# One batch for the last matrix product of a gated mix, with the top-8 taken from the gate pass's own rows and the chosen rows transposed by DMA

## The chip, the cores and the metric

The kernel runs on one core of a Trainium2 chip. The metric is the device time of one launch in microseconds; lower is better. The times of one version differ by about 1 us from run to run, so small differences are judged by ratios with an interval.

Engine names in the profile: PE is the tensor engine (PEld its weight loads), DVE the vector engine, ACT the scalar engine, POOL the GpSimd engine, SP the engine whose queue issues most loads. "L771" is a line of that version's program. Line numbers shift by a few from version to version.

## The reference, cut to what matters

```
x = A_x                                             # 2048 tokens x 1024, bf16
g = sigmoid((x * gate_w).sum(-1))                   # a gate for each token
a = 2 * Re(scan(x @ B_bar^T) @ C^T) + x * Dskip     # a diagonal complex recurrence over the tokens
b = x; for the 8 tokens with the largest x @ w_r:
      b[token] += silu(x_sel @ w_gate) * (x_sel @ w_up) @ w_down * sigmoid(r_sel)
out = g * a + (1 - g) * b
```

There are two streams. The large one is `a`: a product with B (called s1 below, PSUM tiles `vps`), a scan on DVE, and a product with C (s2, PSUM tiles `zps`). The small one is `b`: choose 8 tokens, gather their rows, and run three matrix products on 8 rows. They read 22 MB of weights. The small stream is threaded between the matmul groups of the large one.

## The kernel before

The program emits matmul groups in a fixed order. Functions in a list `at((block, position), f)` are run after a given group. A position therefore fixes only where something stands in each engine's queue; when it runs is decided by waits. These are the parts that the change and the argument touch:

```python
xpool = ctx.enter_context(tc.tile_pool(name="xpool", bufs=4))   # 4 x tiles in flight
...
def mul_e(b):        # DVE scales x tile b, POOL's queue stores it
    ...
    nc.gpsimd.dma_start(out2d[b * P:(b + 1) * P, :], xt[:])
def skip_d(k):       # DVE: xd = x * Dskip for the two tiles of block k
    for b in (2 * k, 2 * k + 1): ...
def rows(k):
    for b in (2 * k - 2, 2 * k - 1):
        mul_e(b)
        if b + 4 < NTT:
            load_x(b + 4)          # into the buffer that tile b's store must first leave
...
def load_w():        # SP loads a weight slot into each buffer that came free
def moe_slot(s):     # the matmuls of weight slot s; then its buffer is free, and load_w()
...
def fin_b():         # DVE scales the 8 rows y
def scatter_upd():   # POOL adds them to out in DRAM, then SP reads the last tiles back ("ul")
...
at((3, 2.3), lambda: (rows(2), skip_d(2), dve_scan(3, 0, 8)))
at((3, 6.5), lambda: (skip_d(3), dve_post(3, 0, 8)))          # dve_post makes H, which s2 reads
at((9, 0.1), lambda: last_m(1))
at((9, 2.95), lambda: (fin_b(), scatter_upd(), last_scan(1)))
pos = [(3, 4.9)] * 2 + ... + [(8, 1.9)] * 4 + [(9, 2.9)] * 3  # where each weight slot is used
```

`rows(2)` stores x tiles 2 and 3 and then loads tiles 6 and 7 into the same two buffers. `skip_d(3)` needs tiles 6 and 7. The last two entries of `pos` are the product with w_down, called y, in two batches.

Of the kernel before, what the change touches and what calls it, by code (L numbers as in the profile page):

```python
# [9 lines left out]
ALU = mybir.AluOpType  # L10
# [14 lines left out]
def kernel(  # L25
# [45 lines left out]
    X = {}  # L71
    BT = [const.tile([P, KD, NP_], BF16, name=f"BT{pl}") for pl in range(2)]
    CT = [const.tile([P, NCT, D], BF16, name=f"CT{pl}") for pl in range(2)]
# [60 lines left out]
    nc.gpsimd.iota(ramp[:], pattern=[[1, LC]], base=0, channel_multiplier=0, allow_small_or_imprecise_dtypes=True)  # L134
    jrow8 = small.tile([8, NTT, 8], F32, name="jrow8")
    nc.gpsimd.iota(jrow8[:], pattern=[[P, NTT], [0, 8]], base=0, channel_multiplier=0, allow_small_or_imprecise_dtypes=True)
    M = {}
    rg = small.tile([P, KD, 32], BF16, name="rg")
    nc.gpsimd.memset(rg[:], 0.0)
    ones16 = small.tile([NTT, 8], BF16, name="ones16")  # L140
    nc.gpsimd.memset(ones16[:], 1.0)
    for i, v in enumerate((B_w_r, gate_w)):
# [290 lines left out]
    nc.vector.tensor_scalar(out=rs4[:, 1, 0, :], in0=rot[:, 1, 1, :], scalar1=-1.0, scalar2=None, op0=ALU.mult)  # L433

    s1x(1, 0)
    tab_arg(1)
    tab_abs(1)
    vb_ps = ps_m.tile([P, 2, NCT], BF16, name="vb_ps", tag="m")
    for i in range(2):
        nc.tensor.transpose(vb_ps[:, i, :], vrow[:, 3 + i, :], ident[:NCT, :NCT])  # L440
    nc.vector.tensor_copy(rg[:, :, 0:2].rearrange("p k t -> p t k"), vb_ps[:])
# [36 lines left out]

    rcb = small.tile([P, NTT], BF16, name="rcb")
    gcol = small.tile([P, NTT], F32, name="gcol")  # L480
# [10 lines left out]
    def gate_cols():  # L491
        zt = ps_m.tile([P, 4, P], BF16, name="zt", tag="m")
        for tq in range(4):
            nc.tensor.transpose(zt[:, tq, :], M["zrb"][:, tq * P:(tq + 1) * P], ident[:])
        zv = zt[:].rearrange("p t (j s) -> p j t s", s=32)
        zb = small.tile([P, NTT], BF16, name="zb")
        nc.scalar.copy(out=zb[:].rearrange("p (j t) -> p j t", t=4), in_=zv[:, :, :, 1])
        gb = sigm(small, zb[:], [P, NTT], "gc")
        nc.scalar.copy(out=gcol[:], in_=gb[:])
        nc.scalar.copy(out=rcb[:].rearrange("p (j t) -> p j t", t=4), in_=zv[:, :, :, 0])  # L500
        ob = small.tile([P, NTT], BF16, name="ob")
        nc.scalar.activation(out=ob[:], in_=gb[:], func=ACT.Copy, scale=-1.0, bias=1.0)
        nc.scalar.copy(out=omgcol[:], in_=ob[:])
        M["aT"] = small.tile([P, NFC // 4, 4, 32], BF16, name="aT", tag="va")
        nc.gpsimd.memset(M["aT"][:], 0.0)
# [11 lines left out]
    def sel_a():  # L517
        rT_ps = ps_m.tile([NTT, P], BF16, name="rT_ps", tag="m")
        nc.tensor.transpose(rT_ps[:], rcb[:], ident[:])
        rT = rowp.tile([NTT, P], F32, name="rT", tag="row8")  # L520
        nc.scalar.copy(out=rT[:], in_=rT_ps[:])
        M["rT"] = rT

    def sel_a2():
        rT = M["rT"]
        mA = rowp.tile([NTT, NSEL], F32, name="mA")
        iA = rowp.tile([NTT, NSEL], U32, name="iA")
        nc.vector.max(out=mA[:], in_=rT[:])
        nc.vector.max_index(out=iA[:], in_max=mA[:], in_values=rT[:])
        iAf = rowp.tile([NTT, NSEL], F32, name="iAf")  # L530
        nc.vector.tensor_copy(iAf[:], iA[:])
        mm = rowp.tile([NTT, 2, NTT, NSEL], BF16, name="mm", tag="mg")
        eyeb = ident[:NTT, :NTT].unsqueeze(2).to_broadcast([NTT, NTT, NSEL])
        nc.vector.tensor_tensor(out=mm[:, 0], in0=mA[:].unsqueeze(1).to_broadcast([NTT, NTT, NSEL]), in1=eyeb, op=ALU.mult)
        nc.vector.tensor_tensor(out=mm[:, 1], in0=iAf[:].unsqueeze(1).to_broadcast([NTT, NTT, NSEL]), in1=eyeb, op=ALU.mult)
        M["mm"] = mm

    def sel_b():
        mm = M["mm"]
        fl_ps = ps_m.tile([NSEL, 2, NTT * NSEL], F32, name="fl_ps", tag="m")  # L540
        for k in range(2):
            nc.tensor.matmul(fl_ps[:, k, :], lhsT=ones16[:], rhs=mm[:, k].rearrange("k j s -> k (j s)"), start=True, stop=True)
        fl = rowp.tile([NSEL, 2, NTT * NSEL], F32, name="fl", tag="gr0")
        nc.scalar.copy(out=fl[:], in_=fl_ps[:])
        M["fl"] = fl

    def sel_b2():
        fl = M["fl"]
        cv = fl[:, 0, :]
        ci = rowp.tile([NSEL, NTT * NSEL], F32, name="ci", tag="mg")  # L550
        nc.vector.tensor_tensor(out=ci[:], in0=fl[:, 1, :], in1=jrow8[:].rearrange("p j s -> p (j s)"), op=ALU.add)
        gm = rowp.tile([NSEL, NSEL], F32, name="gm")
        kx = rowp.tile([NSEL, NSEL], U32, name="kx")
        nc.vector.max(out=gm[:], in_=cv)
        nc.vector.max_index(out=kx[:], in_max=gm[:], in_values=cv)
        kxf = rowp.tile([NSEL, NSEL], F32, name="kxf")
        nc.vector.tensor_copy(kxf[:], kx[:])
        dtmp = rowp.tile([NSEL, 2, NSEL], F32, name="dtmp")
        nc.vector.tensor_tensor(out=dtmp[:, 0, :], in0=kxf[:], in1=ident[:NSEL, :NSEL], op=ALU.mult)
        nc.vector.tensor_tensor(out=dtmp[:, 1, :], in0=gm[:], in1=ident[:NSEL, :NSEL], op=ALU.mult)  # L560
        dsel = rowp.tile([NSEL, 2], F32, name="dsel")
        nc.vector.reduce_sum(out=dsel[:], in_=dtmp[:], axis=AX)
        eq = rowp.tile([NSEL, NTT * NSEL], F32, name="eq", tag="gr1")
        nc.vector.tensor_scalar(out=eq[:], in0=ramp[:NSEL, 0:NTT * NSEL], scalar1=dsel[:, 0:1], scalar2=None, op0=ALU.is_equal)
        nc.vector.tensor_tensor(out=eq[:], in0=eq[:], in1=ci[:], op=ALU.mult)
        tokf = rowp.tile([NSEL, 1], F32, name="tokf")
        nc.vector.reduce_sum(out=tokf[:], in_=eq[:], axis=AX)
        idx_c = small.tile([NSEL, 1], I32, name="idx_c")
        nc.vector.tensor_copy(idx_c[:], tokf[:])
        M["idx_c"] = idx_c  # L570
        xsel = rowp.tile([NSEL, D], BF16, name="xsel", tag="row8")
        nc.gpsimd.indirect_dma_start(out=xsel[:], out_offset=None, in_=x2d, in_offset=bass.IndirectOffsetOnAxis(ap=idx_c[:, :1], axis=0))
        M["xsel"] = xsel
        M["dsel"] = dsel
    def sel_c():
        xsel = M["xsel"]
        xselT_ps = ps_m.tile([P, KD, NSEL], BF16, name="xselT_ps", tag="m")
        for dc in range(KD):
            nc.tensor.transpose(xselT_ps[:, dc, :], xsel[:, dc * P:(dc + 1) * P], ident[:NSEL, :NSEL])
        xselT = M["xsel32"]  # L580
        nc.scalar.copy(out=xselT[:, :, 0:NSEL], in_=xselT_ps[:])
        M["xselT"] = xselT
        M["rs_e"] = sigm(rowp, M["dsel"][:, 1:2], [NSEL, 1], "rs")
# [40 lines left out]
    def load_w():  # L624
        while nload[0] < NS and free_w:
            s = nload[0]
            tag = free_w.pop(0)
            if s < NGU // 2:
                h, dc = divmod(s, KD)
# [3 lines left out]
            else:  # L633
                w = const.tile([P, 2, 2, D], BF16, name="wd", tag=tag)
                for i in range(2):
# [10 lines left out]
    def moe_slot(s):  # L646
        for i in range(2):
            moe_item(2 * s + i, wq[s][0][:, i])
        free_w.append(wq.pop(s)[1])
        load_w()  # L650
# [190 lines left out]
    at((3, 1.9), sel_c)  # L841
    at((3, 3.9), sel_d)
    at((3, 1.2), lambda: dve_m(3, 0, 8))
    at((3, 2.3), lambda: (rows(2), skip_d(2), dve_scan(3, 0, 8)))
    at((3, 4.2), lambda: (sel_c2(), sel_d2()))
    at((3, 2.2), lambda: rows_e(2))
# [10 lines left out]
    at((5, 3.4), lambda: fin(6))  # L857
    at((5, 2.6), lambda: (dve_m(5, 0, 8), dve_scan(5, 0, 8)))
    at((5, 2.5), lambda: skip_d(4))
    at((6, 2.2), lambda: skip_x(8))  # L860
# [22 lines left out]
    at((8, 2.5), lambda: fin(10))  # L883
    at((9, 2.92), fin_a)
    at((8, 3.95), lambda: fin(11))
    at((9, 0.0), lambda: (skip_d(7), last_post(0, 0, NCT)))
    at((9, 0.1), lambda: last_m(1))
    at((9, 2.95), lambda: (fin_b(), scatter_upd(), last_scan(1)))
    at((9, 2.5), lambda: fin(12))
# [3 lines left out]

    pos = [(3, 4.9)] * 2 + [(4, 1.9)] * 3 + [(5, 1.9)] * 3 + [(6, 1.9)] * 3 + [(6, 5.9)] * 3 + [(7, 0.9)] * 2 + [(8, 1.9)] * 4 + [(9, 2.9)] * 3
    for s in range(NW // 2):
# [10 lines left out]
    for n, (m, k) in enumerate(blocks):  # L906
        free_w.extend(fill.get(n, ()))
        load_w()
        if k is None:
# [45 lines left out]
```

## Time and profile before

| | before |
|---|---|
| time, median of the first 3 runs | 249.81 us (249.35 to 250.25) |
| span of the profiled run | 248.3 us |
| PE busy | 242.7 us, 98% |
| DVE busy | 227.0 us, 91% |
| PE's clock | full (mean granted 1.000) |

The page's busy part (busy us, share of the span, instructions) of the kernel before:

```profile
PE 242.7 (98%) x1414; PEld 115.6 (47%) x1414; DVE 227.0 (91%) x231; ACT 117.4 (47%) x203; POOL 33.6 (14%) x50
```

A busy PE is not by itself a PE at its limit, so the order matters. These are lines of the chain of waits of the kernel before, in order of time: start, length (both in us), engine, tile, line, and number of instructions.

```profile
66.83 3.45 PE zps L771 x16
70.28 0.15 PE rT_ps L519
...
101.93 0.28 PE xselT_ps L579 x8
...
109.23 0.27 PE zs_ps L595 x8
109.50 3.56 PE vps L266 x16
...
207.16 1.86 PE y L672 x64
...
226.39 1.42 PE y L672 x48
...
238.28 6.96 PE zps L787 x48
```

From 61 to 245 us the chain is PE alone, one piece after another. A group of 16 large matmuls takes 3.45 us in a stream. After an interruption by matmuls with smaller weights (128 x 8 for `zs_ps`) it takes 3.56 us; after one with weights of 128 x 128 (`zt`, which stands just before the first line shown, and `aT_ps` at 203.3 us) it takes 3.45 us. The tiny transposes (`rT_ps`, `xselT_ps`), the gate product `zs_ps` and the two `y` pieces are the interruptions that the change attacks.

A line of a timeline gives start, length, engine, line, operation, tile, and in brackets the idle time before and what ended it.

Two waits of DVE at the end of the kernel before, from its view of waits (who waited for whom; us in total, times, longest):

```profile
DVE xt L760 <- DMA ul<-out_dram: 2.6, 1, 2.6
DVE yc L696 <- ACT yc L691: 2.6, 1, 2.6
```

### The profile page before, as it was taken

To read this page: it belongs to the slowest core of one execution; us is meant where nothing else is said; L and a number is where in the kernel's file an instruction comes from. 1 tells how busy PE (TensorE), PEld (TensorE's weight loads), DVE (VectorE), ACT (ScalarE), POOL (GpSimd) and SP (SyncE) were. 2 spreads that over 40 slices of the span, in tenths; PEclk is the share of its full clock that TensorE was granted. 3 is DMA by queue.
4 is the path that set the end of the run, shared out by engine and by line. 5 is a ranking of instruction groups with operands and counts; after the bars stand their busy time and mean duration, and the time that the engine had idled before them with its cause. 6 is when DMAs were issued, how large, how long until landed. Compare 5 with 4: busy or idle time off the path is not lost.

```text
span 248.3 us, 3608 instructions
## 1 busy us (share of the span) xinstructions
PE 242.7 (98%) x1414; PEld 115.6 (47%) x1414; DVE 227.0 (91%) x231; ACT 117.4 (47%) x203; POOL 33.6 (14%) x50
## 2 busy tenths in 40 slices
PE   7899999999999999999999999999999999999995
PEld 5664444444444444444444444444444445445453
DVE  0899999999999999999999999999999999995954
ACT  3599973333345322282354571235267445537421
POOL 4000000000100003151402050100100211011810
PEclk9999999999999999999999999999999999999999
DMA  7999999999760000077976989877599972993053
GB/s 170 214 201 213 223 228 202 261 220 255 225 220 0 3 0 0 7 187 210 340 212 225 343 252 300 279 240 291 156 313 317 374 157 59 308 309 45 3 118 96
DMA packets 64193, 48.25 MB, mean 194 GB/s; under 512 B 49568, under 2 KB 51232, under 8 KB 64176
## 3 DMA queue, kind: packets, MB, share of 16 engines
q1 hardware_dynamic: 59120, 37.23, 55.5%
q0 software_dynamic: 3424, 7.90, 14.8%
q10 hardware_dynamic: 1632, 2.89, 3.8%
q8 instruction: 11, 0.18, 0.3%
q14 instruction: 6, 0.05, 0.1%
HBM read 27.55 MB, written 8.40 MB: 145 GB/s over the span
## 4 chain that ended last, share of the span: by engine, by line
PE 84%; DVE 7%; DMA 4%; SPq 3%; issue 0%; ACT 0%; DVEq 0%
PE zps L771 42%; PE vps L266 32%; DMA X<-in_A_x_dram 4%; PE zps L787 3%; PE pgu L660 3%; SPq L80 2%; PE vps L282 1%; PE y L672 1%; DVE U L302 1%; DVE U L313 1%; DVE H L340 1%; DVE U L338 1%; DVE H L336 1%; PE zr L487 1%; DVE S2tab L252 1%; DVE Ctab L251 1%
## 5 line engine op out<-in xcount | busy, mean ns | idle before, releaser
L771 PE MATMUL zps<-CT,H 128*128 128x512 bf16 x480 | 105.5, 379 | 0.0
L266 PE MATMUL vps<-X,BT 128*128 128x512 bf16 x480 | 105.1, 379 | 0.0
L266 PEld LDWEIGHTS <-BT 128*128 128x128 bf16 x480 | 46.4, 98 | 56.6 <-PE pgu L660 0.7
L771 PEld LDWEIGHTS <-H 128*128 128x128 bf16 x480 | 46.2, 98 | 56.3 <-issue 1.5
L313 DVE TENSOR_TENSOR_SCAN U<-d,U 128x2048 bf16<-128x2048 f32 (+2 forms) x22 | 62.0, 2860 | 1.0 <-DVE U L304 0.5
L273 ACT CAST V<-vps 128x512 bf16<-128x512 f32 x60 | 32.2, 588 | 56.3 <-PE vps L266 56.3
L776 ACT ACTIVATE ot<-zps,gcol 128x512 bf16<-128x512 f32 x30 | 20.6, 687 | 54.1 <-PE zps L771 54.1
L797 POOL DMA_DIRECT2D out_dram<-ot x14 | 13.0, 931 | 34.4 <-ACT ot L776 24.0
L303 DVE TENSOR_TENSOR V<-V,nTi 128x4096 bf16<-128x4096 bf16 (+2 forms) x11 | 16.7, 1517 | 0.5
L304 DVE TENSOR_TENSOR U<-U,V 128x4096 bf16<-128x4096 bf16 (+2 forms) x11 | 16.7, 1516 | 0.4
L302 DVE TENSOR_TENSOR U<-V,T2tab 128x4096 bf16<-128x4096 bf16 (+2 forms) x11 | 16.6, 1509 | 0.4
L338 DVE TENSOR_TENSOR U<-U,S2tab 128x4096 bf16<-128x4096 bf16 x7 | 16.0, 2292 | 0.2
L340 DVE TENSOR_TENSOR H<-H,U 128x4096 bf16<-128x4096 bf16 x7 | 16.0, 2292 | 0.2
L336 DVE TENSOR_TENSOR H<-U,Ctab 128x4096 bf16<-128x4096 bf16 x7 | 16.0, 2283 | 0.0
L745 ACT CAST zps<-xd 128x512 f32<-128x512 bf16 (+1 forms) x25 | 14.2, 575 | 3.2 <-ACT xt L732 2.9
L709 POOL DMA_DIRECT2D xt<-in_A_x_dram x12 | 7.1, 592 | 62.7 <-DMA out_dram<-xt 31.5
L732 ACT ACTIVATE xt<-xt,omgcol 128x1024 bf16<-128x1024 bf16 x12 | 13.8, 1146 | 0.0
L371 DVE TENSOR_TENSOR_SCAN U<-D,U 128x1024 bf16<-128x1024 f32 x4 | 8.9, 2271 | 0.1
L282 PE MATMUL vps<-X,BT 128*128 128x256 bf16 x64 | 7.5, 273 | 0.9 <-DMA X<-in_A_x_dram 0.6
L727 DVE TENSOR_TENSOR xd<-xt,Dbc 128x1024 bf16<-128x1024 bf16 x12 | 7.7, 682 | 0.3 <-ACT V L273 0.3
L282 PEld LDWEIGHTS <-BT 128*128 128x128 bf16 x64 | 6.1, 98 | 2.4 <-issue 0.7
L660 PE MATMUL pgu<-wgu,xsel 128*32 128x448 bf16 x128 | 7.2, 354 | 0.0
(161 smaller groups left out, 152.7 us busy)
## 6 DMA issues: line engine op xcount, KB each, us to landing
wgu<-in_B_w_gate_dram SPq DMA_DIRECT2D x16, 448.0 KB, 6.5
wgu<-in_B_w_up_dram SPq DMA_DIRECT2D x16, 448.0 KB, 5.8
wd<-in_B_w_down_dram SPq DMA_DIRECT2D x12, 512.0 KB, 7.6
out_dram<-ot POOLq DMA_DIRECT2D x14, 256.0 KB, 5.8
xt<-in_A_x_dram POOLq DMA_DIRECT2D x12, 256.0 KB, 4.2
out_dram<-xt ACTq DMA_DIRECT2D x10, 256.0 KB, 5.3
xt<-in_A_x_dram SPq DMA_DIRECT2D x4, 256.0 KB, 3.5
out_dram<-xt POOLq DMA_DIRECT2D x4, 256.0 KB, 3.4
```

What stands on the lines that cost most here:

```text
L266: nc.tensor.matmul(o, lhsT=BT[pl][:, dc, ct * P:(ct + 1) * P], rhs=X[m][:, dc, k0 * LC:k1 * LC], start=(dc == 0), stop=(dc == KD - 1))
L273: nc.scalar.copy(out=V[k][:, :, ct, :], in_=vp[m, ct][:, :, kk, :])
L282: nc.tensor.matmul(vps[:, pl, c, :], lhsT=BT[pl][:, dc, ct * P:(ct + 1) * P], rhs=X[0][:, dc, k * LC:(k + 1) * LC], start=(dc == 0), stop= ...
L302: nc.vector.tensor_tensor(out=u, in0=v, in1=T2tab[:, :, c0:c1, :], op=ALU.mult)
L303: nc.vector.tensor_tensor(out=v, in0=v, in1=bc(nTi, c0, c1), op=ALU.mult)
L304: nc.vector.tensor_tensor(out=u, in0=u, in1=V[k][:, ::-1, c0:c1, :], op=ALU.add)
L313: nc.vector.tensor_tensor_scan(out=fl, data0=d0[:, c0:c1, :].rearrange("p c t -> p (c t)"), data1=fl, initial=0.0, op0=ALU.mult, op1=ALU.add)
L336: nc.vector.tensor_tensor(out=h, in0=g, in1=bc(Ctab, c0, c1), op=ALU.mult)
L338: nc.vector.tensor_tensor(out=g, in0=g, in1=S2tab[:, :, c0:c1, :], op=ALU.mult)
L340: nc.vector.tensor_tensor(out=h, in0=h, in1=G[k][:, ::-1, c0:c1, :], op=ALU.add)
L771: nc.tensor.matmul(zps[:], lhsT=H[k][:, pl, ct, tl * P:(tl + 1) * P], rhs=CT[pl][:, ct, dsl], start=(fresh and ct == 0 and pl == 0), stop= ...
L776: nc.scalar.activation(out=ots[b][:, dsl], in_=zps[:], func=ACT.Copy, scale=gcol[:, b:b + 1])
```

## The change

Its intent has two halves. The **y half** does the product with w_down in one batch, with B's space as room for weights once B has been used, and puts the chosen rows' gate product beside it. The **selection half** takes the top-8 directly from the router rows of the gate pass (4 rows of 512 instead of 16 rows of 128, which needed a transpose on PE), merges 32 instead of 128 candidates with one matmul instead of two, and transposes the gathered rows by DMA instead of by PE. The diff, cut to its core:

```diff
     def sel_a():
-        rT_ps = ps_m.tile([NTT, P], BF16, name="rT_ps", tag="m")
-        nc.tensor.transpose(rT_ps[:], rcb[:], ident[:])
-        rT = rowp.tile([NTT, P], F32, name="rT", tag="row8")
-        nc.scalar.copy(out=rT[:], in_=rT_ps[:])
+        rT = rowp.tile([P, 2 * LC], F32, name="rT", tag="row8")
+        nc.scalar.copy(out=rT[:], in_=M["zrb"][:])
 ...
+        M["xsel"] = rowp.tile([32, D], BF16, name="xsel", tag="row8")
+        nc.gpsimd.memset(M["xsel"][:], 0.0)
 ...
     def sel_c():
-        for dc in range(KD):
-            nc.tensor.transpose(xselT_ps[:, dc, :], xsel[:, dc * P:(dc + 1) * P], ident[:NSEL, :NSEL])
-        nc.scalar.copy(out=xselT[:, :, 0:NSEL], in_=xselT_ps[:])
+        nc.sync.dma_start_transpose(xselT[:], xsel[:])
 ...
-    at((3, 3.9), sel_d)
+    at((8, 3.88), sel_d)
 ...
-    at((9, 2.92), fin_a)
+    at((8, 3.92), fin_a)
-    at((9, 2.95), lambda: (fin_b(), scatter_upd(), last_scan(1)))
+    at((9, 0.95), lambda: last_scan(1))
+    at((9, 0.15), lambda: (sel_c2(), sel_d2(), fin_b(), scatter_upd()))
 ...
-    pos = ... + [(8, 1.9)] * 4 + [(9, 2.9)] * 3
+    pos = ... + [(8, 3.9)] * 7
 ...
+        if n == 7:
+            for pl in range(2):
+                t = const.tile([P, 4, 2, D], BF16, name="wdb", tag=f"BT{pl}")
+                free_w.extend(((t, 0), (t, 1)))
```

The diff also moves the two transposes of the gate vectors ahead of a matmul group at the start, and one `skip_d` behind its block's `dve_m`.

More of the change, by code (lines that the diff above doesn't have):

```diff
@@ L71 @@
     X = {}
-    BT = [const.tile([P, KD, NP_], BF16, name=f"BT{pl}") for pl in range(2)]
+    BT = [const.tile([P, KD, NP_], BF16, name=f"BT{pl}", tag=f"BT{pl}") for pl in range(2)]
     CT = [const.tile([P, NCT, D], BF16, name=f"CT{pl}") for pl in range(2)]
@@ L134 @@
     nc.gpsimd.iota(ramp[:], pattern=[[1, LC]], base=0, channel_multiplier=0, allow_small_or_imprecise_dtypes=True)
-    jrow8 = small.tile([8, NTT, 8], F32, name="jrow8")
-    nc.gpsimd.iota(jrow8[:], pattern=[[P, NTT], [0, 8]], base=0, channel_multiplier=0, allow_small_or_imprecise_dtypes=True)
+    jrow8 = small.tile([8, 4, 8], F32, name="jrow8")
+    nc.gpsimd.iota(jrow8[:], pattern=[[2 * LC, 4], [0, 8]], base=LC, channel_multiplier=0, allow_small_or_imprecise_dtypes=True)
     M = {}
@@ L139 @@
     nc.gpsimd.memset(rg[:], 0.0)
-    ones16 = small.tile([NTT, 8], BF16, name="ones16")
-    nc.gpsimd.memset(ones16[:], 1.0)
+    ones8 = small.tile([P, 8], BF16, name="ones8")
+    nc.gpsimd.memset(ones8[:], 1.0)
     for i, v in enumerate((B_w_r, gate_w)):
@@ L433 @@
     nc.vector.tensor_scalar(out=rs4[:, 1, 0, :], in0=rot[:, 1, 1, :], scalar1=-1.0, scalar2=None, op0=ALU.mult)
+    vb_ps = ps_m.tile([P, 2, NCT], BF16, name="vb_ps", tag="m")
+    for i in range(2):
+        nc.tensor.transpose(vb_ps[:, i, :], vrow[:, 3 + i, :], ident[:NCT, :NCT])
     s1x(1, 0)
@@ L437 @@
     tab_abs(1)
-    vb_ps = ps_m.tile([P, 2, NCT], BF16, name="vb_ps", tag="m")
-    for i in range(2):
-        nc.tensor.transpose(vb_ps[:, i, :], vrow[:, 3 + i, :], ident[:NCT, :NCT])
     nc.vector.tensor_copy(rg[:, :, 0:2].rearrange("p k t -> p t k"), vb_ps[:])
@@ L477, in sigm @@
         return e
-    rcb = small.tile([P, NTT], BF16, name="rcb")
     gcol = small.tile([P, NTT], F32, name="gcol")
@@ L499, in gate_cols @@
         nc.scalar.copy(out=gcol[:], in_=gb[:])
-        nc.scalar.copy(out=rcb[:].rearrange("p (j t) -> p j t", t=4), in_=zv[:, :, :, 0])
         ob = small.tile([P, NTT], BF16, name="ob")
@@ L525, in sel_a2 @@
         rT = M["rT"]
-        mA = rowp.tile([NTT, NSEL], F32, name="mA")
-        iA = rowp.tile([NTT, NSEL], U32, name="iA")
+        mA = rowp.tile([P, NSEL], F32, name="mA")
+        iA = rowp.tile([P, NSEL], U32, name="iA")
         nc.vector.max(out=mA[:], in_=rT[:])
         nc.vector.max_index(out=iA[:], in_max=mA[:], in_values=rT[:])
-        iAf = rowp.tile([NTT, NSEL], F32, name="iAf")
-        nc.vector.tensor_copy(iAf[:], iA[:])
-        mm = rowp.tile([NTT, 2, NTT, NSEL], BF16, name="mm", tag="mg")
-        eyeb = ident[:NTT, :NTT].unsqueeze(2).to_broadcast([NTT, NTT, NSEL])
-        nc.vector.tensor_tensor(out=mm[:, 0], in0=mA[:].unsqueeze(1).to_broadcast([NTT, NTT, NSEL]), in1=eyeb, op=ALU.mult)
-        nc.vector.tensor_tensor(out=mm[:, 1], in0=iAf[:].unsqueeze(1).to_broadcast([NTT, NTT, NSEL]), in1=eyeb, op=ALU.mult)
+        iAf = rowp.tile([P, NSEL], F32, name="iAf")
+        nc.vector.tensor_scalar(out=iAf[:], in0=iA[:], scalar1=-float(LC), scalar2=None, op0=ALU.add)
+        mm = rowp.tile([P, 2, 4, NSEL], BF16, name="mm", tag="mg")
+        eyeb = ident[:, 0:P:32].unsqueeze(2).to_broadcast([P, 4, NSEL])
+        nc.vector.tensor_tensor(out=mm[:, 0], in0=mA[:].unsqueeze(1).to_broadcast([P, 4, NSEL]), in1=eyeb, op=ALU.mult)
+        nc.vector.tensor_tensor(out=mm[:, 1], in0=iAf[:].unsqueeze(1).to_broadcast([P, 4, NSEL]), in1=eyeb, op=ALU.mult)
         M["mm"] = mm
@@ L539, in sel_b @@
         mm = M["mm"]
-        fl_ps = ps_m.tile([NSEL, 2, NTT * NSEL], F32, name="fl_ps", tag="m")
-        for k in range(2):
-            nc.tensor.matmul(fl_ps[:, k, :], lhsT=ones16[:], rhs=mm[:, k].rearrange("k j s -> k (j s)"), start=True, stop=True)
-        fl = rowp.tile([NSEL, 2, NTT * NSEL], F32, name="fl", tag="gr0")
+        fl_ps = ps_m.tile([NSEL, 2, 4 * NSEL], F32, name="fl_ps", tag="m")
+        nc.tensor.matmul(fl_ps[:].rearrange("p k n -> p (k n)"), lhsT=ones8[:], rhs=mm[:].rearrange("p k j s -> p (k j s)"), start=True, stop=True)
+        fl = rowp.tile([NSEL, 2, 4 * NSEL], F32, name="fl", tag="gr0")
         nc.scalar.copy(out=fl[:], in_=fl_ps[:])
         M["fl"] = fl
+        M["xsel"] = rowp.tile([32, D], BF16, name="xsel", tag="row8")
+        nc.gpsimd.memset(M["xsel"][:], 0.0)
     def sel_b2():
@@ L549, in sel_b2 @@
         cv = fl[:, 0, :]
-        ci = rowp.tile([NSEL, NTT * NSEL], F32, name="ci", tag="mg")
+        ci = rowp.tile([NSEL, 4 * NSEL], F32, name="ci", tag="mg")
         nc.vector.tensor_tensor(out=ci[:], in0=fl[:, 1, :], in1=jrow8[:].rearrange("p j s -> p (j s)"), op=ALU.add)
@@ L562, in sel_b2 @@
         nc.vector.reduce_sum(out=dsel[:], in_=dtmp[:], axis=AX)
-        eq = rowp.tile([NSEL, NTT * NSEL], F32, name="eq", tag="gr1")
-        nc.vector.tensor_scalar(out=eq[:], in0=ramp[:NSEL, 0:NTT * NSEL], scalar1=dsel[:, 0:1], scalar2=None, op0=ALU.is_equal)
+        eq = rowp.tile([NSEL, 4 * NSEL], F32, name="eq", tag="gr1")
+        nc.vector.tensor_scalar(out=eq[:], in0=ramp[:NSEL, 0:4 * NSEL], scalar1=dsel[:, 0:1], scalar2=None, op0=ALU.is_equal)
         nc.vector.tensor_tensor(out=eq[:], in0=eq[:], in1=ci[:], op=ALU.mult)
@@ L570, in sel_b2 @@
         M["idx_c"] = idx_c
-        xsel = rowp.tile([NSEL, D], BF16, name="xsel", tag="row8")
-        nc.gpsimd.indirect_dma_start(out=xsel[:], out_offset=None, in_=x2d, in_offset=bass.IndirectOffsetOnAxis(ap=idx_c[:, :1], axis=0))
-        M["xsel"] = xsel
+        xsel = M["xsel"]
+        nc.gpsimd.indirect_dma_start(out=xsel[0:NSEL, :], out_offset=None, in_=x2d, in_offset=bass.IndirectOffsetOnAxis(ap=idx_c[:, :1], axis=0))
         M["dsel"] = dsel
@@ L576, in sel_c @@
         xsel = M["xsel"]
-        xselT_ps = ps_m.tile([P, KD, NSEL], BF16, name="xselT_ps", tag="m")
-        for dc in range(KD):
-            nc.tensor.transpose(xselT_ps[:, dc, :], xsel[:, dc * P:(dc + 1) * P], ident[:NSEL, :NSEL])
         xselT = M["xsel32"]
-        nc.scalar.copy(out=xselT[:, :, 0:NSEL], in_=xselT_ps[:])
+        nc.sync.dma_start_transpose(xselT[:], xsel[:])
         M["xselT"] = xselT
@@ L627, in load_w @@
             tag = free_w.pop(0)
+            if isinstance(tag, tuple):
+                t, i0 = tag
+                w = t[:, 2 * i0:2 * i0 + 2]
+            elif s >= NGU // 2:
+                w = const.tile([P, 2, 2, D], BF16, name="wd", tag=tag)[:]
             if s < NGU // 2:
@@ L633, in load_w @@
             else:
-                w = const.tile([P, 2, 2, D], BF16, name="wd", tag=tag)
                 for i in range(2):
@@ L648, in moe_slot @@
             moe_item(2 * s + i, wq[s][0][:, i])
-        free_w.append(wq.pop(s)[1])
+        tag = wq.pop(s)[1]
+        if not isinstance(tag, tuple):
+            free_w.append(tag)
         load_w()
@@ L841 @@
     at((3, 1.9), sel_c)
-    at((3, 3.9), sel_d)
+    at((8, 3.88), sel_d)
     at((3, 1.2), lambda: dve_m(3, 0, 8))
     at((3, 2.3), lambda: (rows(2), skip_d(2), dve_scan(3, 0, 8)))
-    at((3, 4.2), lambda: (sel_c2(), sel_d2()))
     at((3, 2.2), lambda: rows_e(2))
@@ L857 @@
     at((5, 3.4), lambda: fin(6))
-    at((5, 2.6), lambda: (dve_m(5, 0, 8), dve_scan(5, 0, 8)))
-    at((5, 2.5), lambda: skip_d(4))
+    at((5, 2.6), lambda: (dve_m(5, 0, 8), skip_d(4), dve_scan(5, 0, 8)))
     at((6, 2.2), lambda: skip_x(8))
@@ L892 @@
     at((10, 0.5), lambda: (add_upd(NTT - 2), add_upd(NTT - 1)))
-    pos = [(3, 4.9)] * 2 + [(4, 1.9)] * 3 + [(5, 1.9)] * 3 + [(6, 1.9)] * 3 + [(6, 5.9)] * 3 + [(7, 0.9)] * 2 + [(8, 1.9)] * 4 + [(9, 2.9)] * 3
+    pos = [(3, 4.9)] * 2 + [(4, 1.9)] * 3 + [(5, 1.9)] * 3 + [(6, 1.9)] * 3 + [(6, 5.9)] * 3 + [(7, 0.9)] * 2 + [(8, 3.9)] * 7
     for s in range(NW // 2):
```

## The prediction

> **What bounds the kernel now.** The tensor engine, by sheer work. The page gives PE 98% busy of a 248.3 us span at a granted clock of 9 tenths or more throughout. In the chain of waits PE has 84%; from 61.1 us (gate pass) to 245.2 us every piece is PE, without a wait between. In a long run the big matmuls cost 0.216 us each. Before that the chain runs through DVE (37 to 55 us) and the transposing load of X; after 245.3 us it is the last eviction and store. DVE (91%) is almost never idle, but ahead: in the timeline the state blocks H end 1.5 to 28 us before PE reads them. So time falls only where PE instructions or interruptions of the dense stream go.
>
> **What an interruption costs.** In the chain 16 big matmuls after an interruption take 3.56 us, in a stream 3.45 us: 0.11 us for the return. y takes 1.86 us for 64 and 1.42 us for 48 matmuls: 0.027 us each and about 0.13 us for entering. The Trainium skill, "TensorEngine Tiling (Array Packing)", section Key Properties, says that changing the tiling mode drains the engine; holes of 0.4 us in weight loading around these groups agree.
>
> **What goes from PE (chain of waits), us:**
> - router column's transpose (0.15 + 0.11 return): 0.26
> - eight transposes of the chosen rows, now a DMA transpose (0.28 + 0.11): 0.39
> - two short index matmuls become one (0.20): 0.06
> - chosen rows' gate product (0.27) moves next to the y batch: 0.1 to 0.2
> - two y batches become one: one entry, one return, 0.25
> - two transposes of the gate vectors (0.13) move into PE's 0.57 us wait for X at 11.4 us: 0.15, if the start-up chain shifts too.
>
> Sum about 1.2 us, all on the critical path. The products themselves stay.
>
> **What is added or moved elsewhere.** DVE: top-8 over 512 instead of 128 elements (two instructions of 0.28 us; estimate 0.7 us each), repaid by merging 32 instead of 128 candidates; net about zero at 76 to 96 us, where H has 5 us in hand. Late, DVE no longer waits 2.6 us for the y copy (timeline, 227 us), but nothing on PE waited for it. DMA: rows are gathered at 96.6 us and land 3.7 us later; a transposing load takes 5.2 us, so the transposed rows are there near 107 us; PE wants them at 113 us. Weights: all seven w_down slots must land by 214 to 217 us, where the single y batch runs. With B's space they are issued from 181 to 190 us; DMA moved only 157 and 59 GB/s from 199 to 211 us, against 310 to 370 around it, so the 3 MB that came late before fit there and land near 211 us. Little slack, but slack.
>
> **Predicted: 248.6 us, 247.8 to 249.5** (0.5% faster than 249.81). Chances: faster by over 2%: 0.02; within 2%: 0.95; slower by over 2%: 0.03.
>
> **In the profile afterwards.** Right if PE busy falls by about 1 us without a new PE wait; the chain shows one y piece of about 3.1 us near 214 us preceded by the gate product, and no transposes near 70 and 102 us; the gate-vector transposes sit in the wait at 11.4 us; the DMA row shows one filled stretch near the end instead of two. Wrong if PE waits for w_down or the transposed rows, or DVE pieces appear after 61 us.
>
> **What would make it wrong.** The burst of weights delays x tiles or output stores so that presets or output buffers come late; the DMA transpose is held in its queue and blocks the gate/up loads behind it; DVE's new order delays H; the start-up chain doesn't move.

## More of the kernel before

```profile
113.59 0.34 SPq L632 DMA_DIRECT2D wgu<-in_B_w_gate_dram  x1
113.73 0.56 POOL L722 DMA_DIRECT2D out_dram<-xt  x1 [3.88 <-DVE xt L721]
118.56 0.55 POOL L709 DMA_DIRECT2D xt<-in_A_x_dram  x1 [3.08 <-DMA out_dram<-xt]
121.99 0.57 POOL L709 DMA_DIRECT2D xt<-in_A_x_dram  x1 [1.96 <-DMA out_dram<-xt]
124.43 0.33 SPq L632 DMA_DIRECT2D wgu<-in_B_w_gate_dram  x1
125.16 1.27 DVE L727 TENSOR_TENSOR xd<-xt,Dbc 128x1024 bf16<-128x1024 bf16 x2
```

Each reload of an x tile (L709) waits for the store of the tile that was in the buffer. The last reload is issued at 121.99 us and lands 3.3 us later, at 125.3 us. DVE starts the second of its two products at about 125.75 us (the two end at 126.43, and one takes 0.68). No wait appears, but only half a microsecond is left.

## The result, and the profile after

| | before | changed |
|---|---|---|
| median time, 4 runs each | 249.68 us (249.35 to 250.25) | 251.37 us (250.95 to 251.55) |
| ratio | 1 | 1.0063, interval 1.0040 to 1.0086 |
| span of the profiled run | 248.3 us | 249.5 us |

A ratio here and below is the mean time of one kernel's runs over that of the kernel before in the same rounds, so it is not quite the ratio of the quoted medians. The changed kernel was not run in the rounds of the experiments; they are compared with it through the kernel before. The change is 0.6% slower, where 0.5% faster was predicted. It is inside the 2% class and outside the predicted range. The granted clock was 0.996 to 1.000 in the four runs, and the run at 1.000 was the slowest (251.55 us), which speaks against the clock as the cause.

The busy part of the page of the changed kernel:

```profile
PE 240.0 (96%) x1380; PEld 115.6 (46%) x1404; DVE 227.7 (91%) x231; ACT 117.6 (47%) x201; POOL 34.4 (14%) x51
```

It counts 1404 weight loads, ten fewer than before (the 9 transposes and one short matmul that are gone), but only 1380 matmuls: 24 matmul records are missing from this trace. The busy time of PE is therefore no measure of the saving, and positions in time are used instead. This is the end of PE's timeline in the changed kernel:

```profile
215.15 0.66 PE L671 MATMUL y<-wd,aT 128*32 128x256 bf16 x16
215.74 20.89 PE L770 MATMUL zps<-CT,H 128*128 128x512 bf16 x94
238.47 7.12 PE L786 MATMUL zps<-CT,H 128*128 128x512 bf16 x47 [1.84 <-DVE H L385]
```

The group before the last ended at 236.6 us (215.74 plus 20.89). In the kernel before it ended at 238.3. PE had thus won about 1.65 us by then, of which 0.35 us came from a shorter start, and it lost 1.84 us in a single wait for H. The view of waits names where DVE lost its time:

```profile
DVE xd L726 <- DMA xt<-in_A_x_dram: 3.9, 1, 3.9
DVE xt L759 <- DMA ul<-out_dram: 2.5, 1, 2.5
```

The wait for the y copy is gone, as predicted. A new wait of 3.9 us for an x tile has come. In the timeline of the changed kernel, these lines answer to those shown of before:

```profile
111.68 0.35 SPq L630 DMA_DIRECT2D wgu<-in_B_w_gate_dram  x1
114.33 0.56 POOL L721 DMA_DIRECT2D out_dram<-xt  x1 [3.84 <-DVE xt L720]
122.04 0.55 POOL L708 DMA_DIRECT2D xt<-in_A_x_dram  x1 [5.95 <-DMA out_dram<-xt]
122.51 0.33 SPq L630 DMA_DIRECT2D wgu<-in_B_w_gate_dram  x1
123.15 0.92 POOL L708 DMA_DIRECT2D xt<-in_A_x_dram  x1
130.00 0.69 DVE L726 TENSOR_TENSOR xd<-xt,Dbc 128x1024 bf16<-128x1024 bf16 x1 [3.85 <-DMA xt<-in_A_x_dram]
```

PE is about 2 us earlier here, so it frees its first two weight buffers earlier, and 1.8 MB of weight loads leave at 111.68 us instead of 113.59. DVE is 0.6 us later, so the x stores leave at 114.33 us instead of 113.73. The weights now have a lead of 2.65 us where they had 0.14. The first store took 7.4 us to land instead of 4.5, and the reload of tile 6 waited for it. The second store took as long as before (6.7 us against 6.8), but the reload of tile 7 stands behind that of tile 6 in POOL's queue. It was then issued behind the next weight loads (122.51 us), and took 6.8 us instead of 3.3. Tile 7 landed 4.7 us later than before (130.0 us against 125.3): 1.2 us by its later issue and 3.5 us by its slower transfer. DMA queue statistics from 114 to 117 us show the crowding (packets, MB, share of the 16 engines' time; q1 carries SP's loads, q0 carries POOL's transfers). First before, then changed:

```profile
q1 hardware_dynamic: 136, 0.44, 60.0%
q0 software_dynamic: 35, 0.13, 11.5%
```

```profile
q1 hardware_dynamic: 265, 0.86, 90.5%
q0 software_dynamic: 5, 0.00, 0.2%
```

The late DVE has a second consequence. The scaling of y stands behind three products in DVE's queue, so the scatter of y left at 232.18 us. Lines of the chain of waits of the changed kernel:

```profile
231.32 0.54 DVE yc L695
...
232.18 6.83 DMA out_dram<-yc,idx_c
...
239.06 3.76 DMA ul<-out_dram
```

The read-back (`ul`) came at 242.8 us. The last five output stores were then issued one after another from 244.6 to 246.5 us, while in the kernel before the last one left at 245.8.

The product that completes the H for PE's last group, from the timelines of DVE (kernel before first, then the changed kernel):

```profile
235.96 0.69 DVE L385 TENSOR_TENSOR H<-H,U 128x1024 bf16<-128x1024 bf16 x1
```

```profile
237.73 0.69 DVE L385 TENSOR_TENSOR H<-H,U 128x1024 bf16<-128x1024 bf16 x1
```

### The profile page after: what moved, and what is told of

It is laid out like the page before. It is cut to its first block, busy times and chain, and to the rows that moved or that the text cites. A ratio compares the mean times of both kernels' runs of the same rounds, so it can differ in the third digit from the quotient of the medians. Undisturbed runs are those within 1.5% of the kernel's fastest.

```text
span 249.5 us, 3565 instructions
## 1 busy us (share of the span) xinstructions
PE 240.0 (96%) x1380; PEld 115.6 (46%) x1404; DVE 227.7 (91%) x231; ACT 117.6 (47%) x201; POOL 34.4 (14%) x51
## 4 chain that ended last, share of the span: by engine, by line
PE 82%; DVE 7%; DMA 6%; SPq 1%; issue 1%; ACT 0%; DVEq 0%; ACTq 0%
PE vps L266 42%; PE zps L770 33%; DMA out_dram<-yc,idx_c 3%; PE pgu L659 3%; DMA BT<-in_A_B_im_dram 2%; PE vps L282 2%; DVE U L371 2%; DMA ul<-out_dram 2%; PE y L671 1%; SPq L80 1%; PE zr L486 1%; DVE xd L726 1%; DVE xt L759 1%; ACT yc L690 0%; DVE U L361 0%
## 5 line engine op out<-in xcount | busy, mean ns | idle before, releaser
L266 PEld LDWEIGHTS <-BT 128*128 128x128 bf16 x480 | 46.6, 98 | 57.2 <-PE pgu L659 1.1
L786 PE MATMUL zps<-CT,H 128*128 128x256 bf16 (+1 forms) x47 | 7.1, 307 | 1.9 <-DVE H L385 1.8
L754 POOL DMA_INDIRECT out_dram<-yc,idx_c x1 | 5.3, 5293 | 17.9 <-DVE yc L695 17.9
```

Of the source, the lines that this page charges most:

```text
L266: nc.tensor.matmul(o, lhsT=BT[pl][:, dc, ct * P:(ct + 1) * P], rhs=X[m][:, dc, k0 * LC:k1 * LC], start=(dc == 0), stop=(dc == KD - 1))
```

## The experiments

**Theory A.** The saved PE time moved the weight loads ahead of the x stores. Tile 7 came late, DVE stood for 3.85 us, and the delay reached PE through H and the output through the scatter. **Theory B.** DVE's own added work, the wider top-8 and the clearing on POOL, makes H late. **Theory C.** The single y batch, with its burst of weights and its reordered end, costs the time. All outputs are right.

### e1: the two skip products after H

```diff
-    at((3, 6.5), lambda: (skip_d(3), dve_post(3, 0, 8)))
+    at((3, 6.5), lambda: (dve_post(3, 0, 8), skip_d(3)))
```

> The changed kernel, with one DVE order swapped: the two skip products of tiles 6 and 7 come after the three H products of block 3 instead of before them. Same work, same DMA. Theory A (late x tile): in the changed kernel DVE stood 3.85 us at 126 us for x tile 7, whose load left late, and only that made H of the last block late, so that PE waited 1.84 us at 236.6 us. Then here DVE's wait at 126 us is gone (under 0.5 us), PE waits for no H at the end, and the time is 248.0 to 249.0 us, under the kernel before. Theory B (DVE's extra work): the top-8 over 512 elements and the clearing on GpSimd lengthened DVE's stretch at 75 to 78 us from 1.2 to 2.7 us, and this makes H late. Then the PE wait stays near 1.8 us and the time near 251.4. Theory C (the single y batch with its burst of weights and the earlier scatter costs the time at the end): time near 251 too.

Measured: 248.95 us (247.67 to 250.37, 6 runs) against 249.53 for the kernel before; ratio 0.9966, interval 0.9931 to 1.0. No work and no transfer was taken away; only DVE's order changed. From its timelines of DVE and PE:

```profile
130.62 2.29 DVE L340 TENSOR_TENSOR H<-H,U 128x4096 bf16<-128x4096 bf16 x1
132.83 1.28 DVE L726 TENSOR_TENSOR xd<-xt,Dbc 128x1024 bf16<-128x1024 bf16 x2
...
237.04 7.11 PE L786 MATMUL zps<-CT,H 128*128 128x512 bf16 x48
```

No bracket follows either product or the last PE group, so neither waited. The reloads in this run left at 121.81 and 122.92 us, as late as in the changed kernel. They were merely no longer waited for. The interval of the ratio lies clear of the changed kernel's (from 1.0040). Theory B fails here: DVE did all its added work and PE waited for no H. Theory C fails as well, as the y batch is still single.

### e2: the first two weight slots one group later

```diff
-    pos = [(3, 4.9)] * 2 + ...
+    pos = [(3, 5.9)] * 2 + ...
```

> The changed kernel, with the first two gate/up slots one matmul group (3.46 us) later on PE, so that the weight loads they release leave at about 115.1 us instead of 111.7, that is after the first store of an x tile (114.3 us), as in the kernel before (113.6 against 113.7). Theory A with its mechanism (the store, and then the reload into the same buffer, queue behind weight loads that leave earlier because PE is now earlier): the stores land in 5 to 7 us instead of 6.7 to 7.4, tile 7 is reloaded before the next weights leave at 122.5 us, DVE's wait shrinks from 3.85 us to under 1.5, PE's wait to under 0.3, time 248.3 to 249.7. Theories B and C: time near 251.4, PE wait 1.8.

Measured: 248.70 us (248.35 to 249.88, 6 runs); ratio 0.9978, interval 0.9953 to 1.0003. From the timeline of this version:

```profile
114.36 0.56 POOL L721 DMA_DIRECT2D out_dram<-xt  x1 [3.84 <-DVE xt L720]
114.97 0.34 SPq L630 DMA_DIRECT2D wgu<-in_B_w_gate_dram  x1
117.47 0.55 POOL L708 DMA_DIRECT2D xt<-in_A_x_dram  x1 [1.36 <-DMA out_dram<-xt]
121.43 0.57 POOL L708 DMA_DIRECT2D xt<-in_A_x_dram  x1 [2.50 <-DMA out_dram<-xt]
122.35 0.33 SPq L630 DMA_DIRECT2D wgu<-in_B_w_gate_dram  x1
```

The store leaves at the same time as in the changed kernel (114.36 against 114.33 us), but now ahead of the weights, and it lands in 2.8 us instead of 7.4. Both reloads leave before the next weights. DVE's wait for an x tile and PE's wait for H are both gone. DVE and POOL ran the same instructions at the same times as in the changed kernel until the store landed (DVE's scan began at 116.40 us against 116.36), so they did not cause the 7.4 us. The delay of the stores is thus a matter of which transfer leaves first. No run separates the weights that leave at 112 us from those at 122.5 us, which passed the reload of tile 7.

### e3 and e4: each half alone

e3 is the kernel before with the y half; e4 is the changed kernel with the y half taken back:

```diff
 e4, against the changed kernel:
-    at((8, 3.88), sel_d)
+    at((3, 3.9), sel_d)
-    pos = ... + [(8, 3.9)] * 7
+    pos = ... + [(8, 1.9)] * 4 + [(9, 2.9)] * 3
 ... fin_a, fin_b, scatter and last_scan back to their old places; B's space unused
```

> The kernel before with the y half alone: one y batch, B's space for weights, gate product of the chosen rows beside it, and the reordered end; the old selection stays. Theory A: PE is only 0.4 us earlier at 113 us, so the stores still leave with the weights: no DVE wait for an x tile over 1 us, no PE wait, one y piece; PE saves about 0.6 us: 248.6 to 249.5 us. Theory C: slower than before, 250.5 or more.

> The changed kernel with the y half taken back: new selection (top-8 of the gate pass's rows, rows transposed by DMA), old two y batches and old end. Theory A: PE is about 1.2 us earlier and the stores 0.6 us later at 113 us, so weights leave 2 us ahead of the stores: DVE waits 2 to 4 us for x tile 7, part of it hidden in the old 2.6 us wait for the y copy, PE waits 0.5 to 1.8 us at the end: 249.8 to 251.2 us. Theory B: DVE 1 us late at 78 us, otherwise no wait: 249 to 250 with no DVE wait for an x tile. Theory C: faster than before, about 248.8.

Measured: e3 249.35 us (247.94 to 250.55), ratio 0.9983, interval 0.995 to 1.0017, so no difference is shown. e4 250.48 us (250.06 to 250.81), ratio 1.0031, interval 1.001 to 1.0051, so slightly slower. The waits for an x tile and for H, e4 first:

```profile
DVE xd L726 <- DMA xt<-in_A_x_dram: 3.7, 1, 3.7
PE zps L786 <- DVE H L385: 0.5, 1, 0.5
```

```profile
DVE xd L733 <- DMA xt<-in_A_x_dram: 1.2, 1, 1.2
```

The selection half brings the whole wait for tile 7. In e4 that delay takes up the old 2.6 us wait for the y copy, which is no longer seen. The y half alone has a small wait (1.2 us, where under 1 was expected) and none on PE. In this one profile e3 had also lost 1.56 us at the start in a wait for a B tile. That PE waits only 0.55 us in e4 is not owed to that idle gap. DVE begins the `xd` products of the last block at 222.03 us in e4 and in the changed kernel alike, and the gap is gone in both: used up in one, removed in the other. H ends at 237.86 us in e4, from this line of DVE's timeline, against 238.42:

```profile
237.17 0.69 DVE L385 TENSOR_TENSOR H<-H,U 128x1024 bf16<-128x1024 bf16 x1
```

These 0.56 us are three small instructions and a wait of 0.21 us, which the y half moved there. The other 0.74 us are PE's: without the y half it is ready for H at 237.37 us instead of 236.63.

### e5: clearing on ACT

```diff
-        nc.gpsimd.memset(M["xsel"][:], 0.0)
+        nc.scalar.activation(out=M["xsel"][:], in_=Dbc[:32, :], func=ACT.Copy, scale=0.0)
```

> The changed kernel, with the clearing of the chosen rows' buffer done by the scalar engine (a copy scaled by 0) instead of GpSimd. In the changed kernel two tiny DVE instructions lasted 0.9 to 1.0 us, exactly while GpSimd's clearing of 0.95 us ran. If the two engines exclude each other there, these fall back to under 0.3 us and DVE's selection stretch from 2.66 to about 1.8 us. Theory A: the x stores leave 0.8 us earlier (113.5 us) but still behind the weights (111.7), so tile 7 still comes late: DVE's wait stays over 2 us, PE's at 0.5 to 1.8 us, time 250.2 to 251.4. Theory B (what is left of it: DVE's own extra work decides): time falls by the full 0.8 us or more, under 250.2, with the x wait as it was.

Measured: 250.46 us (249.25 to 251.38) against 249.75; ratio 1.0017, interval 0.9981 to 1.0053. In the changed kernel two tiny DVE instructions had been long while POOL cleared the buffer; here they are short. From the two timelines, the changed kernel first:

```profile
77.09 1.00 DVE L527 TENSOR_SCALAR iAf<-iA 128x8 f32<-128x8 uint32 x1
77.11 0.95 POOL L542 MEMSET xsel<- 32x1024 bf16 x1 [5.51 <-DVE iA L525]
77.17 0.92 DVE L530 TENSOR_TENSOR mm<-mA,ident 128x32 bf16<-128x32 f32 x1
```

```profile
76.93 0.17 DVE L527 TENSOR_SCALAR iAf<-iA 128x8 f32<-128x8 uint32 x1
77.02 0.18 DVE L530 TENSOR_TENSOR mm<-mA,ident 128x32 bf16<-128x32 f32 x1
```

This fits the Trainium skill, "SBUF — State Buffer", section "SBUF: two separate sides": it says that VectorE and GpSimd share a port pair which whoever starts first holds for the whole instruction, while the other blocks. The page names, as VectorE's side of such a conflict, an instruction in a two-port mode, or one with two SBUF inputs if the GpSimd instruction reads SBUF, which a clearing does not. Whether L527 ran in a two-port mode no view shows, nor who came first (the records start 0.02 us apart). Shown is that the clearing on POOL cost DVE about 0.8 us. Yet DVE's wait for tile 7 became longer (4.27 us) and PE's wait stayed at 1.67. The interval of the ratio overlaps the changed kernel's, so no gain in time is shown. The earlier DVE arrived earlier at a late tile. What DVE gains upstream of such a wait is lost in the wait.

### e6: scaling and scatter of y ahead of three DVE products

```diff
-    at((9, 0.15), lambda: (sel_c2(), sel_d2(), fin_b(), scatter_upd()))
+    at((9, 0.05), lambda: (sel_c2(), sel_d2(), fin_b(), scatter_upd()))
```

> The changed kernel, with the scaling of y and its scatter ahead of the last block's three DVE products (3.9 us) instead of behind them. Theory A: the wait for x tile 7 and PE's wait for H are untouched (3.9 and 1.8 us), but the scatter leaves at about 228 us instead of 232, the read-back is there by 239 us instead of 242.8, and the last five stores are no longer issued in one queue-bound row: the end after PE's last matmul shrinks by about 0.7 us; time 250.4 to 251.0 against 251.4 for the changed kernel. Were the late H only half of the loss and the scatter's chain the other half, it would fall by 1.5 us or more.

Measured: 251.06 us (249.83 to 252.64) against 249.75; ratio 1.0048, interval 1.0009 to 1.0086. That interval overlaps the changed kernel's, so the gain in time is inconclusive. In the trace the waits stayed (3.3 us for the tile, 1.8 for H), the read-back left at 232.1 us instead of 239.1, and the stretch from PE's last matmul to the end of the span fell from 3.91 to 3.48 us. The late scatter was therefore worth about 0.4 us, less than the 0.7 expected.

### e7: all four together

The edits of e1, e2, e5 and e6, nothing else.

> The changed kernel with all four: first gate/up slots one group later, skip products of block 3 after its H, clearing on the scalar engine, scatter early. Theory A: no DVE wait for an x tile, no PE wait after the start-up, H of the last block at least 2 us ahead; the saved PE time (about 1.5 us against the kernel before) shows whole: 248.0 to 248.7 us against 249.5 for the kernel before. No better than the versions with one mending (248.7 to 249.0) by more than 0.5 us, as PE bounds all of them.

Measured: 248.33 us (247.64 to 250.30) against 249.75; ratio 0.9955, interval 0.9915 to 0.9995. It beats both kernels, the one before by 0.45% (the interval ends just under 1; e9 repeats it). It is not better than e2 by more than the noise, as expected where PE bounds all of them. The chain of its profile is given by the page as:

```profile
PE 95%; DMA 2%; SPq 2%; DVE 0%; issue 0%
```

In the kernel before PE had 84% of the chain, and in the changed kernel 82%, with DVE 7% and DMA 6%.

### e8: the kernel before with only its weight loads earlier

```diff
-    pos = [(3, 4.9)] * 2 + ...
+    pos = [(3, 4.1)] * 2 + ...     # run in the middle of a matmul group, 8 matmuls earlier
```

> The kernel before, with only the first two gate/up slots 8 matmuls (1.7 us) earlier on PE, in the middle of a group: the weight loads they release leave at about 111.9 us instead of 113.6; everything else, the x stores at 113.7 and 114.9 us too, stays. Theory A's mechanism: the stores land later (the first in 6 to 8 us instead of 4.5), the reload of x tiles 6 and 7 goes out at 120 us or later instead of 118.6 (tile 6), and DVE, which found tile 7 just in time before, waits 0.5 to 3 us near 126 us. The time moves little (249.5 to 250.5), as the old 2.6 us wait for the y copy takes up the delay. If the DVE wait comes instead from something else in the change (the DMA transpose, the clearing), the stores land in 4.5 and 6.8 us as before and there is no wait.

Measured: one run, 249.09 us. The weights left at 110.84 us and the first store at 113.21; two lines of its timeline, and then one of its view of waits:

```profile
113.21 0.56 POOL L724 DMA_DIRECT2D out_dram<-xt  x1 [3.88 <-DVE xt L723]
120.47 0.55 POOL L711 DMA_DIRECT2D xt<-in_A_x_dram  x1 [5.52 <-DMA out_dram<-xt]
```

```profile
DVE xd L729 <- DMA xt<-in_A_x_dram: 1.6, 1, 1.6
```

The store took 7.0 us to land instead of 4.5, and DVE waited for tile 7. Nothing of the change is in this kernel: neither the DMA transpose nor the clearing is needed for the wait. PE waited for no H in this trace: DVE's wait for the y copy shrank from 2.6 to 0.5 us and absorbed the delay. The time of this single run, under the 249.5 to 250.5 expected, says nothing more.

### e9, e10, e11: the mended version again

> The version with all four mendings once more, unchanged, as its six times ran from 247.6 to 250.3 us. Theory A, which says PE bounds it from the gate pass to the end: again 248.0 to 248.9 us median, and PE's time from the first matmul of 512 columns to its last (223.6 us from the start of one to the end of the other in the earlier profile) is the same within 0.5 us in every profile; what differs from run to run lies before that, in the waits for the first B and x loads.

> The same kernel, one more profile. PE's time from the first matmul of 512 columns to its last again within 0.5 us of the others; if its total time is over 249.5 us, the start before that is over 1 us longer. Rival: DMA waits in the middle come and go, and PE's dense stretch itself varies by 1 us or more.

> As the run before this one: the dense stretch within 0.5 us of the others, the spread in the start. Rival: the dense stretch varies by 1 us or more.

Measured: e9 248.36 us (247.94 to 249.23, 6 runs) against 249.56, ratio 0.9955, interval 0.9929 to 0.998; e10 248.36 and e11 248.57, one run each. In the four profiles of this version the time from the start of the first 512-column matmul to the end of the last matmul was 228.04, 227.93, 228.13 and 227.93 us. (The expectation of e9 names 223.6 us for the first; that figure was a slip.) The dense stretch is steady, and the time before it was 14.93 to 15.39 us in these profiles, and 14.89 to 15.98 over all thirteen. No profile fell on one of the runs over 249.5 us, so where those lose their time stays open.

## Why the prediction was wrong, point by point

- **PE's saving: right.** The dense stretch was 229.58 us in the kernel before, of which 0.41 us was a wait for X at the gate pass, so 229.17 without it. It is 228.0 in the mended version: 1.0 to 1.2 us saved, where the prediction's items inside this stretch sum to 1.06 to 1.16. In the changed kernel the single y batch with its gate product came at 212.4 us, no transposes are left at 70 and 102 us, and PE did not wait for w_down or the chosen rows.
- **The gate vectors at the start: not shown.** They were to hide in a wait of 0.57 us for X. In the changed profile that wait was not there. In the profiles of e2, e4 and e11 a wait for X of 0.3 to 0.5 us follows them, so there they hid; but the start itself varies by more than 1 us between profiles, which is more than the 0.15 us at stake.
- **DVE's work "about zero": mis-sized.** The stretch of the top-8 grew from 1.18 to 2.66 us, 0.8 of it through POOL's clearing, and the merging shrank from 2.53 to 1.99 us. The net is about +0.9 us. The two wide instructions took 0.69 us each, as estimated.
- **The step that failed:** "DVE (91%) is almost never idle, but ahead: in the timeline the state blocks H end 1.5 to 28 us before PE reads them. So time falls only where PE instructions or interruptions of the dense stream go." The lead was read at H and not at DVE's own inputs. x tile 7 arrived half a microsecond before DVE needed it, by a chain of store, wait and reload that shared the DMA engines with the weight loads. A faster PE moved those loads by 2 us and broke that margin. H of the last block ended at 238.42 us instead of 236.65, 1.8 us later: 3.85 us of waiting and about 0.5 us of added small work, less the 2.6 us of idle time that the change removed. PE was ready at 236.63 us, 1.65 us earlier, and waited 1.84 us. As an estimate from these numbers: in the kernel before a delay at tile 7 had 4.2 us of slack (1.6 of lead and 2.6 of idle time); the earlier PE and the added work left about 2.1 us of it.
- **The risk was named, at the wrong place.** The prediction feared that a burst of weights would delay x tiles, and looked at w_down near 181 to 211 us. PE waited for no w_down slot and DVE for no x tile there. The gate/up loads at 112 us did the harm, and with them the next ones at 122.5 us.
- **"Late, DVE no longer waits 2.6 us for the y copy ... but nothing on PE waited for it": right, and incomplete.** That idle time was slack for delays before it, as e4 and e8 show. Removing it was no loss by itself, since it turned into lead: in e4 it is used up, and H still ends only 0.56 us earlier than in the changed kernel, for another reason.
- **The sum.** In the two profiles, the dense stretch grew from 229.58 to 230.29 us (1.84 us of waiting for H, less 1.13 us won otherwise, of which 0.41 is the wait for X that the changed profile did not have), the start shrank by 0.35 us, and the end after PE's last matmul grew from 3.03 to 3.91 us. About 0.44 us of that end goes away with the early scatter (e6), and also where DVE no longer stands for tile 7 (e1 and e2, 3.47 us each). The other 0.44 us remains in every version that has the new selection, also in e7. It lies behind the last data moved: from there to the end of the span the kernel before takes 1.30 us and e7 1.74. In the packed trace SP's queue passes its closing semaphore waits one by one there, about 0.06 us each; one of them came after the last store had landed in the kernel before, and eight in e7. No run tested this.

## What to carry to other kernels

When a change makes the bounding engine faster, ask which loads its freed buffers release, and which stores and reloads those will now overtake; then read the margin of each input of the next busiest engine, not only the margin of its output. What such an engine can bear is its lead plus the idle time between the late input and the output: 4.2 us here before the change and about 2.1 after it. Of the 2.1 us lost the earlier PE took 1.65. If a late transfer is found, moving its consumer behind work that can be done without it (e1), or moving the competing load behind the urgent one (e2), costs one line and no work.

## What the Trainium skill lacked or had wrong

- "DMA: Bandwidth & Descriptors", section "Queues, rings and completion order", says that each DMA engine goes round-robin between the queues that have work, and drains a whole packet (typically 9 to 17 descriptors, at most 64) from one before it switches. It gives no time for what a queue can lose by this. From 114 to 117 us of the changed kernel two x stores had been issued on POOL's queue (at 114.33 and 115.54 us), and that queue got 5 of the profile's packets and 0.2% of the engines' time while SP's weight loads got 265 packets and 90.5%. That is about 17 for each of 16 engines; if each is one descriptor, which is not shown, the window does not contradict the page. The size of the effect is what these runs add: the 256 KB store landed in 7.4 us, and in 2.8 us when it left first (e2).
- "SBUF — State Buffer", section "SBUF: two separate sides", names the kinds of DVE instruction that contend with GpSimd, but gives a time only for a software DMA beside a copy, and otherwise ratios. Here a DVE instruction on 128 x 8 values lasted 1.00 us beside a GpSimd clearing of 32 x 1024 values (0.95 us), and 0.17 us without it.
- "TensorEngine Tiling (Array Packing)", section Key Properties, says that changing the tiling mode drains the engine, and gives no time for it. The return to full-size matmuls cost 0.11 us (3.56 against 3.45 us for 16) after `zs_ps` with weights of 128 x 8, and nothing after `aT_ps` with weights of 128 x 128. That the mode makes this difference was not tested.
